# A planned schedule laid out anew: instruction order, PSUM banks and the engines of sixteen operations in a gated linear attention feeding a bilinear FFN

## The chip, the cores and the metric

The kernel runs on one core of one Trainium2 chip. The core has five engines that run side by side, each through its own list of instructions in order: TensorE (PE in the profile, with its weight loads as PEld), VectorE (DVE), ScalarE (ACT), GpSimd (POOL) and SyncE (SP, which here only starts transfers). Transfers are started from the lists of SP, POOL or ACT and carried out by 16 DMA engines. The metric is the device time of one execution in microseconds, and the figure that counts is the median over several runs.

## The reference

Four batches, 8 heads, 768 tokens and 48 channels per head. A recurrent attention with a decay per channel, and then a bilinear feed-forward layer on its output:

```python
for t in range(S):                       # S = 768
    state = alpha[:, :, t, :, None] * state + einsum('bhd,bhe->bhde', k[:, :, t], v[:, :, t])
    y[:, :, t] = einsum('bhd,bhde->bhe', q[:, :, t], state)
x = y.transpose(0, 2, 1, 3).reshape(3072, 384)
out = ((x @ w_a) * (x @ w_b)) @ w_out    # 384 -> 1536 -> 384
```

alpha, q and k lie in float32, and so do the weights; the result is 3072 x 384 in float32.

## The kernel before, in words

**Tiling.** The work is cut into six chunks. Chunk c holds 256 tokens (stripe c // 2 of three) of two batches (u = 0 and 1), so 512 tokens of all heads. A partition holds two neighbouring tokens (r = 0, 1), and the 128 partitions are two halves (g = 0, 1) of 64, over each of which the recurrence is written as a masked product; the state is carried from half to half and from stripe to stripe. So the chunks 2 and 3 need the state left by the chunks 0 and 1, and 4 and 5 that of 2 and 3.

**The stages of one chunk.** Load alpha, k, q and v; take the logarithm of alpha and its running sum on PE; two exponentials of it scale k and q (tile QKp); QKp is turned so that channels lie on partitions (tile kqT); PE forms the scores, the state's update and the output y of the attention; y is brought into the layout of the feed-forward layer (tile xT); PE computes a = x w_a and b = x w_b in twelve pieces of 128 columns each, ACT copies a piece of a out of PSUM, DVE multiplies it with the piece of b that still lies in PSUM (tile prod), and PE multiplies prod by w_out for four blocks m of 128 rows, which are copied out and stored. The chunks 0 and 1 turn QKp on PE and keep y in turned form; chunks 2 to 5 turn both QKp and y by DMA transposes that SP starts.

**What sets the order.** Nothing is planned when the kernel is built. The text `PROGRAM` (line 17 on) lists 837 operations, chunk number first, and the loop at line 921 emits them one after the other. Each engine therefore runs its own operations in the order in which the text names them, and an operation waits for the data it reads and for the buffers it overwrites, however long, with all that follows on the same engine behind it. The last letter of many operations is the engine: V for DVE, S for ACT, P for POOL, Y for SP. A number behind a PE operation is its PSUM bank, of which there are eight; `D`, `SB` and `AQ` take that bank and the next one.

The operations that the text below speaks of, with the function that emits them:

- `ld X u E` (load, line 400): load alpha (a), k, q or v of half-chunk u (`*` both; `0a` and `0b` heads 0 to 3 and 4 to 7 of u = 0). `W` and `Wo` (383, 387): load columns of w_a and w_b, rows of w_out, always from POOL.
- `ln` (408, ACT) logarithm; `l2` (414, POOL or DVE) and `lx` (422, DVE) sum the two tokens of a partition; `H`, `L`, `R` (461, 470, 484) split that sum into parts that PE adds exactly; `B`, `A2`, `AQ` (449, 501, 491) the running sums on PE; `Bs` (456, DVE) that of the even tokens.
- `E` (520, ACT) the exponentials, `i` for k and `b` for q; `ra` (506, ACT) 1/alpha; `lv` (513) the level product, k by alpha or q by 1/alpha, for the even tokens; `mk`, `mq` (535, DVE) the scaled k and q.
- `C`, `Ce` (579, 587) turn QKp on PE and copy it out; `T` (595, SP) the same by DMA; `v` (603) copies a v into the padded tile vx, which only chunks 0 and 1 use.
- `dk`, `de` (558, 567) the decay at the ends of the halves; `K`, `KA` (621, 629) the state's update on PE; `k` (642, DVE) the new state.
- `D` (659) scores; `M` (669, DVE) masks them out of PSUM; `Mc` (673, ACT) copies them unmasked and `Mm` (677, DVE) then masks them in place.
- `SB`, `SA`, `Y` (719, 735) the parts of the attention's output on PE; `X` (748) copies it out of PSUM, and `XT` (762, SP) turns it by DMA for chunks 2 to 5.
- `a f u`, `b f u` (774) one piece of the first layer, `as` (780, ACT) the copy of a, `pr` (786, DVE) the product; the copies of a go round three buffers, so that one waits for the product of the third before it.
- `o m half`, `oc` (794, 805) the second layer; `ot`, `otc` (819, 823) copy it out; `st`, `stc` (832, 835) store it.
- `cu`, `cu2`, `cm`, `ci`, `cz`, `cs`, `c1`, `c2`, `c3` (325 to 376): constants and zeros, nearly all on POOL.

Of the kernel before, what the change touches and what calls it, by code (L numbers as in the profile page):

```python
# [33 lines left out]
1: A2 1 6; ln 0; E 1 b; E 1 i
0: K 1 1 4
1: ld k 1 P
0: Wo 0 6; a 3 1 2; b 5 0 7; k 1 1 V
2: ld a * P
1: l2 0 P
0: cs 1 0 P; Wo 6 12; a 5 1 4; as 5 1; b 5 1 5; pr 5 0; pr 5 1  # L40
1: ra 0; H 0 S; ra 1; L 0 V
0: a 11 * 6; b 3 1 1; as 3 1; pr 3 1; as 11 *; a 4 1 4; as 4 1; a 6 * 0; as 6 *
1: A2 0 2; dk * 3
0: b 11 * 0; pr 11 *; b 6 * 7; pr 6 *; b 4 1 5; pr 4 1
1: lv 0 q P; ld v 1 P
2: ld q * P
1: E 0 i; E 0 b; mq 0 V; lv 0 k V; v 0 V; de *; mk 0 V
0: a 2 1 3; a 10 * 4; as 10 *; b 1 1 7; a 1 1 5; b 7 * 2; b 10 * 1; pr 10 *; a 7 * 6
# [84 lines left out]
2: Mm 0 0 V
1: pr 9 1
2: Y 0; X 0 V; XT 0
3: E 1 b; E 0 b
1: o 0 1 -; ot 0 S; st 2 Y; st 0 Y; a 1 1 0; as 1 1; b 4 1 5; pr 4 1; b 1 1 4; a 8 1 6; as 8 1
0: st 1 Y
3: dr
1: pr 1 1; a 10 1 0; as 10 1; b 8 1 5; b 10 1 2; pr 8 1; pr 10 1; o 3 0 6; o 3 1 -  # L140
3: ld k * P; mq 0 V
4: lx V; ra 0
3: E 0 i; lv 1 k P; lv 0 k P; mk 0 V; T 0
2: b 4 * 0; a 4 * 3; a 10 * 7; b 10 * 4; a 5 * 2; as 10 *; pr 10 *
4: R 0
2: a 2 * 7; as 4 *; pr 4 *; b 5 * 4; a 7 * 1; as 5 *; pr 5 *; b 2 * 3; as 2 *; b 7 * 7; as 7 *; pr 7 *
# [65 lines left out]
4: D 1 0 0; Mc 1 0; Mm 1 0 V; SA 0; Y 0; X 0 S
2: st 2 Y; st 1 Y
4: XT 0
3: o 2 0 7; b 7 * 1
4: Y 1; SA 1
5: AQ 3; E 0 b; E 1 b
3: pr 7 *; o 1 0 2
4: X 1 V; XT 1
3: o 1 1 -; o 2 1 -; o 0 0 0; o 0 1 -  # L220
5: E 0 i; ld q * P; ra 0; E 1 i; mk 1 V; lv 0 q P
3: ot 2 V; st 2 Y
4: a 7 * 4; a 0 * 5; as 0 *; b 0 * 6; b 1 * 7
3: ot 0 S
5: mk 0 V; mq 0 V
3: ot 1 V
5: lv 1 q V; mq 1 V
4: pr 0 *; a 1 * 5; as 1 *; pr 1 *; a 6 * 1; a 2 * 2; as 6 *; as 7 *; as 2 *; b 2 * 6; b 10 * 3; b 6 * 4; b 7 * 0; pr 6 *; pr 7 *; a 10 * 1; as 10 *; pr 10 *
# [17 lines left out]
4: o 3 0 1; o 0 0 7; o 1 0 0; o 0 1 -
5: X 1 S; XT 1
3: st 3 Y
4: o 2 0 2; o 2 1 -; o 3 1 -; o 1 1 -; ot 1 V; st 1 Y; ot 0 S
5: a 3 * 3  # L250
4: ot 3 V
5: b 3 * 7
4: st 3 Y; st 0 Y
5: as 3 *; pr 3 *; a 6 * 5; a 0 * 3; as 0 *; a 1 * 4; as 1 *; b 0 * 1; b 1 * 3; pr 1 *; a 11 * 4; pr 0 *; as 6 *; as 11 *
4: ot 2 S; st 2 Y
5: b 6 * 6; pr 6 *; b 11 * 7; pr 11 *; b 7 * 3; a 8 * 0; a 7 * 5; as 8 *; b 8 * 7; pr 8 *; as 7 *; pr 7 *; b 4 * 2; a 5 * 4; a 4 * 1; a 2 * 7; as 2 *; as 4 *
5: pr 4 *; b 2 * 3; pr 2 *; a 9 * 6; b 5 * 7; as 5 *; a 10 * 1; as 9 *; as 10 *; b 10 * 2; pr 5 *; o 0 0 0; b 9 * 6; pr 10 *; o 3 0 3; pr 9 *; o 0 1 -; ot 0 V
# [699 lines left out]
```

## Time and profile before

| | us |
|---|---|
| median of three runs | 197.73 (197.39 to 216.9) |
| the profiled execution | 196.07 |
| its span, first to last instruction | 194.3 |
| PE busy | 182.1 |
| DVE busy | 135.0 |
| ACT busy | 103.9 |
| POOL busy | 57.0 |

One execution was profiled. Its span is 1.77 us shorter than its own device time, and that device time is 1.66 us below the median. In the rows of the profile a line number such as L778 is the line of the kernel, `out<-in` are tiles, `xN` counts instructions; in the lists in order of time the first number is the start in microseconds after the start of the span and the second the length. A bracket behind a row names the idle time of the engine just before it and what ended it. In the view of the waits, the columns are: in total, how often, the longest.

### The profile page before, as it was taken

The numbers are of one execution on the slowest core, as the hardware profiler recorded it, in microseconds if no ns is written. First come the engines' busy times: TensorE is split into PE (matmuls) and PEld (weight loads), VectorE is DVE, ScalarE is ACT, GpSimd is POOL, SyncE is SP. The second block draws the span as 40 slices with busy tenths as digits, with TensorE's granted clock in tenths as the row PEclk, the third lists the DMA queues.
The fourth block names the chain that finished last, engine by engine and source line by source line (L and its number), as shares of the span: only waits on it lengthen the run. The fifth ranks groups of instructions, "written<-read, shape, count | busy, mean of one in ns | idle before, by whom it ended". The sixth has DMA issues, their size and how long they took to land.

```text
span 194.3 us, 5854 instructions
## 1 busy us (share of the span) xinstructions
PE 182.1 (94%) x2498; PEld 111.3 (57%) x2498; DVE 135.0 (69%) x227; ACT 103.9 (53%) x192; POOL 57.0 (29%) x75
## 2 busy tenths in 40 slices
PE   1798898999989999989999999999999999999993
PEld 1577675666667876634556644555544666544463
DVE  4578845999899898767888289885947770343521
ACT  4558676587736769533445645766154733152510
POOL 7997966830750042600331900000300000000000
PEclk9999999999999999999999999999999999999999
DMA  5999999999899975799987599932797005121004
GB/s 139 241 255 206 244 237 261 256 224 269 204 229 214 179 200 134 76 296 196 201 206 182 117 191 216 126 108 55 85 230 140 3 3 120 43 83 40 0 2 162
DMA packets 57882, 30.96 MB, mean 159 GB/s; under 512 B 47824, under 2 KB 54880, under 8 KB 57856
## 3 DMA queue, kind: packets, MB, share of 16 engines
q0 software_dynamic: 19680, 18.09, 48.5%
q1 hardware_dynamic: 38032, 12.41, 30.6%
q8 instruction: 19, 0.31, 0.7%
q10 hardware_dynamic: 144, 0.10, 0.2%
q14 instruction: 7, 0.06, 0.1%
HBM read 25.98 MB, written 4.74 MB: 158 GB/s over the span
## 4 chain that ended last, share of the span: by engine, by line
PE 77%; DMA 8%; POOL 8%; issue 3%; DVE 2%; ACT 1%; POOLq 0%; DVEq 0%; ACTq 0%
PE psum L778 43%; PE psum L800 22%; DMA wa_t<-in_moe_w_a_dram 5%; DMA xT<-ys 3%; PE psum L666 3%; PE psum L716 2%; POOL a_t L405 2%; PE psum L695 1%; PE psum L619 1%; PE psum L690 1%; PE psum L811 1%; PE psum L499 1%; PE psum L585 1%; POOL wa_t L385 1%; POOL wb_t L385 1%
## 5 line engine op out<-in xcount | busy, mean ns | idle before, releaser
L778 PE MATMUL psum<-xT,wb_t 128*128 128x512 bf16 (+1 forms) x270 | 56.7, 337 | 2.2 <-DMA xT<-ys 1.0
L778 PE MATMUL psum<-xT,wa_t 128*128 128x512 bf16 (+1 forms) x270 | 55.8, 337 | 0.0
L800 PE MATMUL psum<-wo_t,prod 128*128 128x384 bf16 x276 | 48.7, 326 | 0.0
L778 PEld LDWEIGHTS <-wb_t 128*128 128x128 bf16 x270 | 25.5, 98 | 22.6 <-issue 1.7
L778 PEld LDWEIGHTS <-wa_t 128*128 128x128 bf16 x270 | 25.8, 98 | 19.7
L800 PEld LDWEIGHTS <-prod 128*128 128x128 bf16 x276 | 26.1, 98 | 17.6 <-issue 0.6
L518 POOL TENSOR_TENSOR q_t<-q_t,ra 128x384 f32<-128x384 f32 x7 | 7.8, 1117 | 69.0 <-ACT ra L511 51.8
L675 ACT ACTIVATE m<-psum 128x1024 bf16<-128x1024 f32 x16 | 16.0, 1022 | 4.8 <-PE psum L666 4.7
L817 DVE COPY ot<-psum 128x384 f32<-128x384 f32 (+1 forms) x9 | 4.7, 530 | 16.1 <-PE psum L800 15.6
L815 ACT ACTIVATE ot<-psum 128x384 f32<-128x384 f32 (+1 forms) x16 | 7.7, 479 | 14.6 <-PE psum L800 12.0
L544 DVE TENSOR_TENSOR QKp<-k_t,invb 128x768 bf16<-128x768 f32 x10 | 10.0, 997 | 1.7 <-ACT invb L533 1.7
L679 DVE TENSOR_TENSOR m<-m,mask 128x1024 bf16<-128x1024 bf16 x16 | 10.9, 684 | 0.2
L671 DVE TENSOR_TENSOR m<-psum,mask 128x1024 bf16<-128x1024 f32 x8 | 9.7, 1218 | 1.7 <-PE psum L666 1.2
L412 ACT ACTIVATE la<-a_t 128x1536 f32<-128x1536 f32 (+2 forms) x9 | 9.5, 1054 | 2.0 <-DMA a_t<-in_alpha_dram 2.0
L544 DVE TENSOR_TENSOR QKp<-q_t,beta 128x768 bf16<-128x768 f32 x10 | 9.5, 949 | 0.0
L666 PE MATMUL psum<-kqT 64*64 64x128 bf16 x384 | 8.8, 219 | 0.2 <-ACT bl L570 0.2
L454 PE MATMUL psum<-la,ut 128*128 128x192 f32 x16 | 4.7, 446 | 4.2 <-ACT la L412 4.1
L405 POOL DMA_DIRECT2D v_t<-in_v_dram x8 | 8.5, 1065 | 0.3 <-issue 0.2
L405 POOL DMA_DIRECT2D a_t<-in_alpha_dram x7 | 7.4, 1063 | 3.0 <-DMA wa_t<-in_moe_w_a_dram 1.8
L518 POOL TENSOR_TENSOR k_t<-k_t,a_t 128x384 f32<-128x384 f32 x6 | 6.3, 1057 | 6.1 <-DMA k_t<-in_k_dram 6.1
L666 PEld LDWEIGHTS <-kqT 64*64 64x64 bf16 x384 | 6.5, 107 | 2.2 <-issue 2.1
L405 POOL DMA_DIRECT2D k_t<-in_k_dram x7 | 7.4, 1062 | 0.0
(269 smaller groups left out, 274.2 us busy)
## 6 DMA issues: line engine op xcount, KB each, us to landing
out_dram<-ot SPq DMA_DIRECT2D x23, 192.0 KB, 4.1
a_t<-in_alpha_dram POOLq DMA_DIRECT2D x4, 768.0 KB, 12.5
k_t<-in_k_dram POOLq DMA_DIRECT2D x4, 768.0 KB, 7.6
q_t<-in_q_dram POOLq DMA_DIRECT2D x3, 768.0 KB, 8.8
v_t<-in_v_dram POOLq DMA_DIRECT2D x4, 384.0 KB, 6.8
a_t<-in_alpha_dram POOLq DMA_DIRECT2D x3, 384.0 KB, 6.2
k_t<-in_k_dram POOLq DMA_DIRECT2D x3, 384.0 KB, 12.9
q_t<-in_q_dram POOLq DMA_DIRECT2D x3, 384.0 KB, 13.3
```

The lines of the kernel that those rows point to most:

```text
L405: eng.dma_start(out=t[:, us, hs].rearrange("p b h r d -> p (b h) (r d)"), in_=src[ch.b0 + us.start:ch.b0 + us.stop, hs, ch.s * 2 * C:(ch.s ...
L412: nc.scalar.activation(out=ch.la[:, us, hs].rearrange("p b h r d -> p (b h r d)"), in_=ch.a[:, us, hs].rearrange("p b h r d -> p (b h r d) ...
L454: nc.tensor.matmul(p[:, 1], lhsT=ut, rhs=ch.la[:, u, hs, r, :], start=(r == 0), stop=(r == 1))
L518: eng.tensor_mul(x, x, by)
L544: eng.tensor_mul(QKp[ch.c % 2][:, u, j, :, hs, :D], src[:, u, hs].rearrange("p h r d -> p r h d"), f)
L666: nc.tensor.matmul(s2[g * HC:(g + 1) * HC, r, p, rk, :], lhsT=ch.kqT[u][rs, 1, rk, 2 * h + p, g * HC:(g + 1) * HC], rhs=queriesT(ch, u, 2 ...
L671: nc.vector.tensor_mul(m.rearrange("p r a k s -> p (r a) (k s)"), ch.s2[u, h].rearrange("p r a k s -> p (r a) (k s)"), maskn(4))
L675: nc.scalar.activation(out=m.rearrange("p r a k s -> p (r a) (k s)"), in_=ch.s2[u, h].rearrange("p r a k s -> p (r a) (k s)"), func=AF.Copy)
L679: eng.tensor_mul(x, x, maskn(4))
L778: nc.tensor.matmul(p, lhsT=(wa_t, wb_t)[w][:, kk, f * 128:(f + 1) * 128], rhs=ch.xT[:, us.start // 2:us.stop // 2, kk].rearrange("p u g s ...
L800: nc.tensor.matmul(op, lhsT=ch.prod[:, f, at:at + C], rhs=wo_t[:, f, :], start=(f == 0), stop=(f == NFF - 1))
L815: nc.scalar.activation(out=o_, in_=i_, func=AF.Copy)
```

## The change

The functions stay as they are; only `PROGRAM` is another text. It holds the same 837 operations but for the engine or queue of sixteen, and nearly every row of it is in another order and names other banks.

The engines and queues that change (chunk number first):

```
copies:         0: Ce 1 1  V -> S     0: ot 1  V -> S     1: v 0  V -> S     1: v 1  V -> S
                4: X 1     V -> S     4: ot 3  V -> S     5: X 1  S -> V     5: ot 3 S -> V     5: otc 1 1  V -> S
level products: 1: lv 0 q  P -> V     2: lv 0 k  V -> P   3: lv 0 k  P -> V   3: lv 0 q  V -> P   5: lv 0 q  P -> V
loads:          3: ld q *  P -> Y     5: ld q *  P -> Y
```

The order, cut to the places that the prediction uses. The start, with the loads of chunk 0 (half a of the heads first for alpha; k of half b last) and the constants on POOL (the masks, the zeros of the states and the identity moved against the loads):

```diff
-0: c1a; cz 0 q V; cz 0 b P; cu; cu2 P; cs 1 m P; ld a 0b Y; ln 0b; B 0b 6; c1; cz 1 q V; cz 0 v V; Bs 0b; ld a 0a Y; ln 0a; B 0a 2; Bs 0a; fill 5 3; ld k 0b Y
-0: ld q 0b Y; E 0b i; E 0b b; mk 0b V; mq 0b V; cus; E 0a i; E 0a b; ld k 0a Y; mk 0a V; ld q 0a Y; mq 0a V; cm 1; ld v 0 P; v 0 S; ld a 1 P; cm 0; ld v 1 P
-0: ld k 1 P; cs 0 m P; ci; C 0 1 7; Ce 0 1 V; c3 V; C 0 0 0; Ce 0 0 V; fill 1 5; dk 0 5; de 0; K 0 0 7; k 0 0 V; D 0 1 5; M 0 1; D 0 0 0; SB 0 2; ln 1; B 1a 4
...
-0: W a 0 256; X 0 S; C 1 0 7; de 1; Ce 1 0 S
...
+0: c1a; ld a 0a Y; cu; cz 0 v V; cm 0; cz 0 b P; cs 0 0 P; cs 1 0 P; ln 0a; cu2 P; B 0a 6; cz 0 q V; c1; Bs 0a; ld v 0 P; ld a 0b Y; ln 0b; B 0b 4; Bs 0b
+0: fill 5 7; c2 P; ld a 1 P; E 0a i; ld q 0b Y; ld k 0a Y; mk 0a V; E 0b b; E 0a b; mq 0b V; cus; ld q 0a Y; mq 0a V; E 0b i; ld k 0b Y; ld q 1 P; ld k 1 P
+0: ci; mk 0b V; C 0 1 2; Ce 0 1 V; C 0 0 1; Ce 0 0 V; dk 0 7; fill 1 2; v 0 S; de 0; K 0 0 0; k 0 0 V; W b 0 256; ld v 1 P; cz 1 b P; cm 1; D 0 1 5; M 0 1
+0: D 0 0 1; cs 0 m P; SB 0 6; ln 1; B 1a 4; Bs 1a; B 1b 0; Mc 0 0; Mm 0 0 V; Bs 1b; E 1a b; E 1a i; mk 1a V; K 0 1 4; E 1b i; E 1b b; Y 0; SA 0; X 0 S; dk 1 3
+0: de 1; mk 1b V; mq 1a V; C 1 0 1; Ce 1 0 S; mq 1b V; v 1 V; C 1 1 0; Ce 1 1 S; k 0 1 V; K 1 0 7; k 1 0 V; W a 0 256; a 1 0 6; a 0 0 4; b 0 0 3; as 0 0
```

The weights, the second sum over pairs (`1: l2 0`), and the loads around it on POOL. In each text these rows are spread over some twenty; here are POOL's own operations in order, from the first load of weights on:

```
before  0:W a 0 256; 1:ld a 1; 0:W a 256 768; 0:W b 0 256; 0:cz 1 b; 0:W b 256 768; 0:c2; 1:ld a 0; 0:W a 768 1536; 0:W b 768 1536; 1:ld q 0; 1:l2 1; 1:ld v 0; 1:ld k 0; 1:ld q 1; 1:ld k 1; 0:Wo 0 6; 2:ld a *; 1:l2 0; 0:cs 1 0; 0:Wo 6 12; 1:lv 0 q; 1:ld v 1; 2:ld q *; 1:lv 1 q; 1:lv 1 k; 2:ld k *; 3:ld a *
after   0:W b 0 256; 0:ld v 1; 0:cz 1 b; 0:cm 1; 0:cs 0 m; 0:W a 0 256; 1:ld a 1; 0:W a 256 768; 1:ld a 0; 0:W b 256 768; 1:ld k 0; 0:W a 768 1536; 0:W b 768 1536; 1:l2 1; 1:ld q 0; 1:l2 0; 1:ld v 0; 1:ld k 1; 1:ld q 1; 0:cs 1 m; 0:Wo 0 6; 2:ld a *; 0:Wo 6 12; 1:ld v 1; 2:ld k *; 1:lv 1 k; 1:lv 1 q; 2:ld q *; 2:ld v *; 3:ld a *
```

PE's own operations between the last piece of a chunk's attention and the first piece of its first layer:

```
chunk 2  before  2:Y 0; 1:o 0 1; 1:a 1 1; 1:b 4 1; 1:b 1 1; 1:a 8 1; 1:a 10 1; 1:b 8 1; 1:b 10 1; 1:o 3 0; 1:o 3 1; 2:b 4 *
         after   2:Y 0; 1:a 1 1; 1:o 0 1; 1:b 4 1; 1:b 1 1; 1:a 8 1; 1:b 8 1; 1:a 10 1; 1:b 10 1; 1:o 3 0; 1:o 3 1; 2:b 10 *
chunk 3  before  3:Y 1; 2:o 3 0; 2:o 2 0; 2:o 1 0; 2:o 2 1; 2:o 3 1; 2:o 1 1; 3:b 0 *
         after   3:SA 1; 2:o 2 0; 2:o 2 1; 2:o 3 0; 4:AQ; 2:o 3 1; 2:o 1 0; 3:a 0 *
chunk 4  before  4:SA 1; 5:AQ; 3:o 1 0; 3:o 1 1; 3:o 2 1; 3:o 0 0; 3:o 0 1; 4:a 7 *
         after   4:Y 1; 3:o 1 0; 3:o 2 1; 3:o 1 1; 3:o 0 0; 3:o 0 1; 4:b 7 *
```

The end of the program, where the two halves of the last block (`oc 1 0`, `oc 1 1`) and the blocks 2 and 3 change places:

```diff
-5: o 2 0 7; o 3 1 -; ot 3 S; st 3 Y; st 0 Y; o 2 1 -; oc 1 1 0 1; ot 2 V; st 2 Y; oc 1 1 1 -; otc 1 1 V; stc 1 1 S; oc 1 0 0 0; oc 1 0 1 -; otc 1 0 S; stc 1 0 Y
+5: oc 1 0 1 -; o 3 1 -; ot 3 V; st 3 Y; o 2 0 4; otc 1 0 S; stc 1 0 Y; st 0 Y; o 2 1 -; ot 2 V; oc 1 1 0 0; oc 1 1 1 -; otc 1 1 S; stc 1 1 S; st 2 Y
```

More of the change, by code (lines that the diff above doesn't have):

```diff
@@ L34 @@
[L34 to L37, printed above, removed]
-2: ld a * P
[L39 to L48, printed above, removed]
@@ new lines @@
+1: ld a 0 P
+0: W b 256 768
+1: ld k 0 P
+0: W a 768 1536; pr 0 0; D 1 1 0; M 1 1; SB 1 1; W b 768 1536; D 1 0 3; Mc 1 0; b 1 0 5; a 3 0 6; a 4 0 7; pr 1 0; Mm 1 0 V; a 5 0 4
+1: ln 0; l2 1 P
+0: as 3 0
+1: H 1 S; L 1 V
+0: SA 1; Y 1; a 2 0 0
+1: ld q 0 P; l2 0 P; ld v 0 P
+0: b 2 0 6; b 3 0 3; pr 3 0; X 1 S; a 5 1 2
+1: A2 1 1
+0: b 5 0 5; as 2 0
+1: H 0 S
+0: as 4 0; as 5 0
+1: L 0 V
+0: pr 2 0; pr 5 0
+1: ld k 1 P; ld q 1 P
+0: cs 1 m P; Wo 0 6
+2: ld a * P
+0: b 3 1 3; a 3 1 7; as 3 1; b 4 0 6; pr 4 0; K 1 1 5
@@ new lines @@
+0: a 1 1 3; as 1 1; Wo 6 12
+1: ld v 1 P
+2: ld k * P
+1: lv 1 k P; lv 1 q P; mq 1 V; mk 1 V
+2: ld q * P; ld v * P
+3: ld a * P
+0: b 1 1 0; pr 1 1; as 0 1; a 8 * 4; as 8 *; pr 8 *; a 9 * 6; b 9 * 1; b 0 1 2; pr 0 1
+1: C 1 0 0
+0: as 9 *; pr 9 *
+1: D 0 1 3; Mc 0 1
+2: ln *
+1: SB 0 4; D 0 0 6; M 0 0
+0: o 3 0 2
+1: C 1 1 3; Ce 1 1 S
+0: o 0 0 6
+1: SA 0; Mm 0 1 V; Y 0; X 0 S; Ce 1 0 V; D 1 1 0
+0: o 3 1 -; ot 3 S
+1: a 2 0 5
+0: o 0 1 -
+1: Mc 1 1; v 1 S; a 11 0 2; as 11 0; b 11 0 7
+2: lx V; R 0; R 1; AQ 3
@@ L133 @@
[L133 to L146, printed above, removed]
@@ new lines @@
+0: st 3 Y; st 0 Y; st 1 Y
+2: Y 1; X 1 S; XT 1
+1: b 9 1 5; o 0 0 6
+3: AQ 3; E 0 i
+1: ot 2 S
+3: E 0 b
+2: SA 0; Y 0; X 0 V; XT 0
+1: pr 9 1; a 1 1 0; as 1 1
+3: E 1 b
+1: o 0 1 -; b 4 1 7; pr 4 1; ot 0 S; b 1 1 2; pr 1 1; a 8 1 5; b 8 1 1; as 8 1; a 10 1 7; b 10 1 0
+3: ld k * P; lv 1 k P; lv 0 k V
+1: o 3 0 2; pr 8 1; as 10 1; pr 10 1
+3: mq 0 V; dr; E 1 i
+4: ln *; ra 0
+1: o 3 1 -; ot 3 S; st 3 Y
+2: b 10 * 3; a 10 * 5; a 1 * 7; a 2 * 2; as 10 *; as 2 *
+3: mk 0 V; mk 1 V; T 0
+2: pr 10 *
@@ L211 @@
-3: pr 10 *
[L212 to L228, printed above, removed]
@@ L246 @@
[L246 to L257, printed above, removed]
@@ new lines @@
+2: st 3 Y; st 1 Y; st 2 Y; st 0 Y
+4: Mc 1 1
+3: b 3 * 7; pr 3 *; b 10 * 2
+4: SB 1 5; SA 0; D 1 0 0; Mc 1 0; Mm 1 0 V; Y 0; X 0 S; XT 0
+3: o 2 0 7; b 7 * 1
+5: AQ 3
+4: SA 1; Mm 1 1 V; Y 1; X 1 S
+3: pr 10 *
+4: XT 1
+3: o 1 0 2
+5: E 1 b; E 0 i; E 1 i; E 0 b; dr
+3: pr 7 *
+5: mk 0 V; lv 1 q V
+3: o 2 1 -; o 1 1 -; ot 1 V; ot 2 V
+5: ld v * P; lv 1 k P
+3: o 0 0 3; o 0 1 -; ot 0 S
+5: lv 0 q V; mq 0 V; T 0
+4: b 7 * 4; b 2 * 0; b 10 * 3; a 2 * 7; a 0 * 2; as 2 *
+5: mq 1 V; mk 1 V
+4: pr 2 *
```

293 lines of the change are left out of this document (135 added, 158 removed).

## The prediction, as it was made before the result

> **What bounds the kernel now.** I read the page first (which engine is full), then the waits of PE alone, then the busy time by stage, and last the lists in order of time around each wait of PE.
>
> ```profile
> span 194.3 us, 5854 instructions
> PE 182.1 (94%) x2498; PEld 111.3 (57%) x2498; DVE 135.0 (69%) x227; ACT 103.9 (53%) x192; POOL 57.0 (29%) x75
> ...
> PE psum L454 <- ACT la L412: 4.1, 1, 4.1
> PE psum L585 <- POOL ident masks.py:199: 1.2, 1, 1.2
> PE psum L778 <- DMA xT<-ys: 1.0, 1, 1.0
> PE psum L504 <- ACT as__632 L784: 0.8, 1, 0.8
> PE psum L778 <- DVE prod L792: 0.6, 1, 0.6
> PE psum L778 <- DVE Sm L651: 0.5, 1, 0.5
> PE psum L619 <- ACT prod L533: 0.5, 1, 0.5
> PE psum L585 <- DVE QKp L544: 0.2, 1, 0.2
> PE psum L666 <- ACT bl L570: 0.2, 1, 0.2
> ...
> 31.00:55.95 24.95, 24.34 (x374) 16.29 (x371) 22.45 (x37) 16.09 (x31) 12.89 (x12) 1.00 1.20 235
> ```
>
> PE is the bound. It is idle for 194.3 - 182.1 = 12.2 us, and the nine rows of its waits hold 9.1 of these. The first two (5.3 us) are the lead-in, before chunk 0 has anything to turn. What remains, 1.0 + 0.8 + 0.6 + 0.5 + 0.5 + 0.2 + 0.2 = 3.8 us, is all that another order can win behind the lead-in, because PE's matmuls are the same in both texts: 1.9% of the median. From 31 to 55.95 DVE is almost as full as PE (22.45 of 24.95 us), so there it is the next bound. A measurement of this kernel can tell about 2% from no change.
>
> **The change part by part.** I summed PE's work in front of each place in the two texts; the places where a chunk passes from attention to first layer lie at the same amount of work. So I ask only which waits go and which come.
>
> *The lead-in.*
>
> ```profile
> 7.55 0.87 ACT L533 ACTIVATE prod<-psum 128x384 f32<-128x384 f32 x2 [0.40 <-DVE psum L459]
> 7.15 0.37 DVE L459 TENSOR_TENSOR psum<-psum,la 128x192 f32<-128x192 f32 x1 [0.91 <-ACT prod L533]
> 9.01 0.59 POOL masks.py:199 TENSOR_SCALAR_AFFINE_SELECT ident<-ident 128x128 bf16<-128x128 bf16 x1
> 9.66 1.05 PE L585 MATMUL psum<-ident,QKp 128*128 128x128 bf16 x16 [1.24 <-POOL ident masks.py:199]
> ```
>
> Before, the first turn waited for the identity (9.01 + 0.59). After, POOL makes it about 0.5 us sooner, but ACT's four exponentials no longer come in pairs: `E 0a b` stands behind `E 0b b`, which needs the second `Bs` (to 7.52). They end near 8.9 instead of 8.4, and the last product, `mk 0b`, near 9.65: the first turn starts at 9.7, as before. `cs 0 m` moves on POOL behind `cm 1` and ends near 12.3, so `SB 0` starts some 0.3 us later; the waits for bl (0.2; the bank of `dk` is another) and for QKp (0.2; `mk 1b` goes ahead) fall away. Taken: +0.1. Bounds: -0.4 (both waits go, nothing comes) to +0.8 (that and another half microsecond on `SB 0`).
>
> *Chunk 0: weights, and copies on ACT.*
>
> ```profile
> 12.10 0.77 POOL L385 DMA_DIRECT2D wa_t<-in_moe_w_a_dram  x1
> ...
> 13.64 0.76 POOL L385 DMA_DIRECT2D wb_t<-in_moe_w_b_dram  x1
> 14.38 0.52 POOL L348 CAST utr<-ut 128x128 fp32r<-128x128 f32 x1
> L376 POOL MEMSET S<- 128x480 f32 x2 | 1.1, 551 | 0.0
> ...
> wa_t<-in_moe_w_a_dram POOLq DMA_DIRECT2D x1, 384.0 KB, 6.9
> wb_t<-in_moe_w_b_dram POOLq DMA_DIRECT2D x1, 384.0 KB, 8.4
> ...
> L591 ACT ACTIVATE kqT<-psum 128x1024 bf16<-128x1024 bf16 x4 | 4.0, 1022 | 0.3 <-PE psum L585 0.2
> L608 ACT ACTIVATE vx<-v_t 128x768 bf16<-128x768 bf16 x1 | 0.8, 843 | 0.4 <-DMA v_t<-in_v_dram 0.4
> ```
>
> On POOL the middle columns of w_a now stand behind two zeroings of the state (0.55 each), `c2` (0.52) and a load of weights (0.76) that came later before; less one small zeroing that goes, that is some 2.3 us, and 2.4 us for those of w_b. They would land near 14.4 + 6.9 = 21.3 and 16.1 + 8.4 = 24.5, where PE wants them at about 21.1 and 24.0: 0.2 and 0.5 us of waiting if the time to landing holds, less if it was mostly queueing. `Ce 1 1`, now on ACT (1.02 us), stands behind `Ce 1 0`, so `D 1 1` waits some 0.4 us, and `Mc 1 0`, behind both and `ln 1`, holds bank 4 for `a 5 0` by another 0.4. These waits do not add up (PE late for one is in time for the next), and the old 0.5 for Sm goes. Taken: +0.3. Bounds: -0.5 (the old wait goes alone) to +1.5 (all come, one after the other).
>
> *The second sum of chunk 1.*
>
> ```profile
> 26.59 1.17 POOL L405 DMA_DIRECT2D a_t<-in_alpha_dram  x1 [1.84 <-DMA wa_t<-in_moe_w_a_dram]
> 28.82 0.52 ACT L466 ACTIVATE lh<-l 128x384 fp32r<-128x384 f32 x1 [0.92 <-POOL l L420]
> 30.08 0.62 PE psum L504 x2
> ```
>
> `1: l2 0` stood on POOL behind the load of chunk 2's alpha, which waited 1.84 us for an older transfer. ACT waited 0.92 for it with `H 0`, and `as 3 1`, queued behind, freed the bank of `A2 0` late: the 0.8 of the list of waits. After, `l2 0` stands ahead of that load and of four more. Gain: -0.8, bounds -0.8 and 0 (if `ln 0`, now early on ACT, comes as late as the pair sum did).
>
> *Chunk 1: the relief of DVE.* DVE loses `Ce 1 1`, two copies of v, one `ot` and `2: lv 0 k`, and gains one level product, `1: lv 0 q`, earlier.
>
> ```profile
> 52.19 1.35 DVE L518 TENSOR_TENSOR q_t<-q_t,ra 128x384 f32<-128x384 f32 x1
> ...
> 53.93 1.35 DVE L518 TENSOR_TENSOR k_t<-k_t,a_t 128x384 f32<-128x384 f32 x1
> 53.84 1.01 POOL L518 TENSOR_TENSOR k_t<-k_t,a_t 128x384 f32<-128x384 f32 x1
> ...
> L518 DVE TENSOR_TENSOR k_t<-k_t,a_t x4: 548/550/1348, 34.8 to 112.8; 128x384 f32<-128x384 f32 x4
> ```
>
> Three of the five stood between 50 and 56 us in the run of DVE that ended in PE's wait of 0.6 for prod: a copy of v, the copy of an output and the level product of k (1.35 alone). Without them that wait goes: -0.6. But PE is then a microsecond ahead, and DVE is nearly full: `pr 7` behind `mq 0`, `M 0 0` ahead of `o 0 0` and `R 1` ahead of `AQ` come out 0.1 to 0.5 us late. I give +0.5 back. Net -0.1; bounds -0.6 and +0.8.
>
> *From attention to the first layer, chunks 2 to 4.*
>
> ```profile
> 78.05 5.30 DMA xT<-ys
> 107.27 5.99 PE psum L800 x36
> 133.49 0.52 PE psum L499 x12
> ...
> 107.31 0.96 DVE L758 CAST ys<-psum 128x768 bf16<-128x768 f32 x1 [0.86 <-PE psum L716]
> 108.30 1.67 SPq L763 DMA_TRANSPOSE xT<-ys  x1
> ...
> L763 SPq DMA_TRANSPOSE xT<-ys x8: 1213/1255/1924, 75.2 to 162.2; - x8
> DMA to landing us min/median/max: 2.7/2.8/2.8
> L756 ACT ACTIVATE ys<-psum 128x768 bf16<-128x768 f32 x5 | 3.9, 808 | 3.0 <-PE psum L716 1.6 <-PE psum L695 1.3
> ```
>
> In chunk 2 the same ten operations cover the same chain: its wait of 1.0 stays. In chunk 3, copy, transpose and landing took 0.96 + 1.67 + 2.8, with the dispatch 5.5 us, under six half outputs (5.99). Now five of them and `AQ` cover it: 5.0 + 0.52 = 5.5, no slack. In chunk 4 the copy moves to ACT: 0.81 + 1.26 + 2.8 + 0.1 = 5.0 under five half outputs, 5.0: no slack, where `AQ` gave 0.5. Taken +0.2 for both; bounds 0, and +2.4 if both transposes take the 5.30 us of chunk 2 instead of 4.1.
>
> *The rest.* The two loads of q leave POOL for SP. POOL is idle then, so nothing is won; on SP they stand ahead of `dl` and `T`, each one more issue, and the scores that need these lie several microseconds of PE's work later. The other moved copies (chunks 4 and 5) have 7.8 us of outputs over them: 0. At the end, the store of block 2 starts a microsecond later than before but ahead of the last half block, whose path (a copy on ACT, then an issue) is the same: 0, at most +0.5.
>
> **The sum.** +0.1 + 0.3 - 0.8 - 0.1 + 0.2 + 0 = -0.3 us. The profiled execution's 196.07 becomes 195.8. Its runs' median stands 1.66 us higher, at 197.73; so I predict a median of 197.4.
>
> **The rivals.**
>
> 1. *The copy of v on ACT waits for its load* (slower). `1: v 0` now stands on ACT ahead of `ra 1`, `as 11` and both `Ce` of chunk 1, and its load has moved on POOL behind `l2 0`, to about 24.5 us (`ln 0` ends near 23 by my sum of ACT's work, `l2 0` takes about 1).
>
> ```profile
> v_t<-in_v_dram POOLq DMA_DIRECT2D x1, 192.0 KB, 12.3
> ```
>
> By that time to landing v comes at 36.8 us, the copy ends at 37.7, and PE, which by the sum of its work wants it at 35.7 for `KA 0`, waits 2.0 us: 199.4. Against it: those 12.3 us were mostly a queue of older transfers, whose sum in front of v is about the same now, so that it would come near 34.3, 0.5 us in time. It decides from a landing at 34.8 on.
>
> 2. *The transposes of chunks 3 and 4 are slow* (slower): +2.2 over my term, 199.6. For it: chunk 2's took 5.30. Against it: that one ran among two large loads, and chunk 3's took 1.67 + 2.8.
>
> 3. *VectorE and GpSimd block each other.* The level product took 1.35 us on DVE beside one on POOL, and 0.55 (the median) alone. In chunk 3 POOL's `lv 1 k` now falls near DVE's `R 0`, `R 1` and the maskings that lead to chunk 2's transpose, where PE waits already. One such meeting costs 0.8: 198.2. Against it: it needs k to land inside three microseconds. The Trainium skill, "SBUF — State Buffer", section "Who interferes with whom", states that a VectorE instruction with two SBUF inputs contends with a GpSimd instruction that reads SBUF, and that the later one blocks; the 1.35 beside 0.55 agrees with that.
>
> 4. *The waits go and none comes back*: 3.8 us less the 1.0 of chunk 2, 194.9. Against it: DVE's 22.45 of 24.95 us.
>
> **How the numbers follow.** My forecast (195.8 to 198.4) 0.53, rival 1 0.17, rival 2 0.10, rival 3 0.08, rival 4 0.12. Faster by over 2%, under 193.8, needs more than all waits behind the lead-in: 0.05. Slower by over 2%, above 201.7, needs rivals 1 and 2 together or weights and v 4 us late, since the upper bounds add up to 0.8 + 1.5 + 0.8 + 2.4 + 0.5: 0.15. Within: 0.80. The range that leaves out 2 in 10 reaches from rival 4 to a little above rivals 1 and 2: 194.6 to 201.3.
>
> **What would show it.** Right: PE's wait at the second `A2` (L504) and the one for prod near 56 gone, PE 0.5 to 1.5 us ahead at the scores of chunk 2, short waits for xT in chunks 3 and 4, no wait for v on ACT. Wrong: `vx` on ACT (L608) idle before it for a transfer, PE waiting for wa_t or wb_t for a microsecond, a gap over 1 us for xT after 100, or PE idle behind DVE in chunks 2 to 5, where I expect none.

## The result, and the profile after

| | us |
|---|---|
| changed kernel, median of four runs | 207.58 (205.55 to 208.6) |
| kernel before beside it, median of four runs | 198.32 (197.39 to 216.9) |
| ratio after / before | 1.047, 95% interval 1.036 to 1.058 |
| profiled execution of the changed kernel, its span | 207.89, 206.0 |

The change makes the kernel about 9 us slower, outside the range of the forecast. Some executions of several kernels, among them seven of the ten of run 7 below and the profiled one of run 5, came 2 to 10% late for a reason that no trace here shows; the ratios leave these out, the medians don't, so from here on the ratio is the figure to trust.

The page of the changed kernel: span, busy times, and PE's busy row and granted clock in 40 slices of 5.15 us.

```profile
span 206.0 us, 5837 instructions
...
PE 186.4 (90%) x2498; PEld 113.7 (55%) x2498; DVE 134.1 (65%) x223; ACT 107.1 (52%) x197; POOL 52.5 (25%) x72
...
PE   2889999999999589999909989999999999999993
...
PEclk9999999999999969999995999999999999999999
```

The span grew by 11.7 us. PE has the same 2498 matmuls, yet 186.4 - 182.1 = 4.3 us more of busy time; the other 7.4 us are idle. So there are two things to find: a wait, and matmuls that run longer. The clock row has the second: two dips, each just behind a hole in PE's row. The waits of PE have the first:

```profile
PE psum L662 <- DMA kqT<-QKp: 8.4, 3, 4.8
PE psum L450 <- ACT la L408: 4.1, 1, 4.1
PE psum L774 <- DMA xT<-ys: 1.0, 1, 1.0
...
```

The scores (L662) wait 8.4 us for kqT, the tile that SP's DMA transposes `T` write; before, there was no such row. In order of time on PE:

```profile
65.86 0.64 PE L662 MATMUL psum<-kqT 64*64 64x128 bf16 x32 [0.25 <-DMA kqT<-QKp]
...
73.02 0.93 PE L662 MATMUL psum<-kqT 64*64 64x128 bf16 x32 [3.34 <-DMA kqT<-QKp]
73.88 2.10 PE L796 MATMUL psum<-wo_t,prod 128*128 128x384 bf16 x6
...
108.56 0.64 PE L662 MATMUL psum<-kqT 64*64 64x128 bf16 x16 [4.85 <-DMA kqT<-QKp]
```

The kernel before reached its first scores of chunk 2 later:

```profile
68.13 0.64 PE L666 MATMUL psum<-kqT 64*64 64x128 bf16 x32
...
71.45 0.62 PE L666 MATMUL psum<-kqT 64*64 64x128 bf16 x32
```

So at 66 us the changed kernel is 2.3 us ahead. It loses 3.3 us at the scores of u = 0 in chunk 2, and 4.85 us at those of u = 1 in chunk 3. Six half-block matmuls behind the first wait take 2.10 us. Six of the same shape take 1.14 in an undisturbed row of the kernel before:

```profile
97.35 1.14 PE L800 MATMUL psum<-wo_t,prod 128*128 128x384 bf16 x6
```

The busy times by stage (last three columns: granted clock, DMA share, GB/s) show the clock at half behind each wait:

```profile
73.00:76.00 3.00, 2.98 (x46) 1.50 (x50) 1.38 (x2) 1.94 (x2) 0.99 (x1) 0.54 0.07 26
...
103.60:108.50 4.90, 0.11 (x14) 0.01 (x2) 1.48 (x2) 0.00 (x0) 1.20 (x1) 0.88 1.03 255
108.50:111.00 2.50, 2.44 (x21) 1.14 (x22) 0.30 (x1) 1.02 (x1) 0.00 (x0) 0.50 0.22 54
```

While PE waits from 103.6 to 108.5 the DMA engines move 255 GB/s. What they move is on SP's list (two transposes, then the stores, and for chunk 3 one transpose that is issued late) and on POOL's:

```profile
60.76 5.20 SPq L592 DMA_TRANSPOSE kqT<-QKp  x2
66.02 2.15 SPq L829 DMA_DIRECT2D out_dram<-ot  x3
...
91.95 0.46 SPq L401 DMA_DIRECT2D q_t<-in_q_dram  x1
92.47 3.15 SPq L829 DMA_DIRECT2D out_dram<-ot  x2
...
98.07 3.82 SPq L592 DMA_TRANSPOSE kqT<-QKp  x1
```

```profile
62.98 1.96 POOL L514 TENSOR_TENSOR q_t<-q_t,ra 128x384 f32<-128x384 f32 x2 [9.70 <-DMA q_t<-in_q_dram]
64.88 1.19 POOL L401 DMA_DIRECT2D k_t<-in_k_dram  x1
...
98.62 1.00 POOL L514 TENSOR_TENSOR q_t<-q_t,ra 128x384 f32<-128x384 f32 x1 [12.87 <-DMA q_t<-in_q_dram]
99.57 2.36 POOL L401 DMA_DIRECT2D k_t<-in_k_dram  x2
```

On POOL in the kernel before, the k load of chunk 3 stood behind a product that waited for ACT's `ra`:

```profile
68.47 0.99 POOL L518 TENSOR_TENSOR q_t<-q_t,ra 128x384 f32<-128x384 f32 x1 [11.26 <-ACT ra L511]
69.41 1.20 POOL L405 DMA_DIRECT2D k_t<-in_k_dram  x1
...
96.60 2.34 POOL L405 DMA_DIRECT2D k_t<-in_k_dram  x2
```

The time from issue to landing of the transposes `T`, first of the kernel before, then of the changed one. The traces give the landing of only some of the eight in each kernel (two in the changed one, those that PE waited for):

```profile
DMA to landing us min/median/max: 4.3/4.4/5.0
```

```profile
DMA to landing us min/median/max: 9.3/9.9/10.4
```

Chunk 2's second transpose is issued at about 63.7 us and lands at 73.0; the 768 KB of k that POOL issues at 64.9 run beside it. Chunk 3's second is issued at 98.07 and lands at 108.5; 1.5 MB of k are issued from 99.57 on, 1.5 us behind it. Before, the same transpose left SP at 93.45, the k loads followed 3.2 us behind it (96.60), and it landed in 5.0 us:

```profile
93.45 2.71 SPq L596 DMA_TRANSPOSE kqT<-QKp  x1
```

So the first collision is a k load that moved ahead, and the second a transpose that fell back, with three stores now ahead of it on SP.

### The profile page after: what moved, and what is told of

Read it like the earlier page. It is cut to its first block, busy times and chain, and to the rows that moved or that the text cites. A ratio compares the mean times of both kernels' runs of the same rounds, so it can differ in the third digit from the quotient of the medians.

```text
span 206.0 us, 5837 instructions
## 1 busy us (share of the span) xinstructions
PE 186.4 (90%) x2498; PEld 113.7 (55%) x2498; DVE 134.1 (65%) x223; ACT 107.1 (52%) x197; POOL 52.5 (25%) x72
## 4 chain that ended last, share of the span: by engine, by line
PE 81%; DMA 14%; DVE 1%; ACT 1%; issue 1%; DVEq 0%
PE psum L774 44%; PE psum L796 20%; DMA kqT<-QKp 10%; PE psum L662 3%; DMA xT<-ys 3%; PE psum L686 2%; PE psum L712 2%; PE psum L581 2%; PE psum L450 2%; PE psum L615 2%; PE psum L691 1%; DMA a_t<-in_alpha_dram 1%; PE psum L807 1%; PE psum L495 1%; PE psum L561 1%
## 5 line engine op out<-in xcount | busy, mean ns | idle before, releaser
L774 PE MATMUL psum<-xT,wb_t 128*128 128x512 bf16 (+1 forms) x270 | 57.4, 342 | 0.0
L796 PE MATMUL psum<-wo_t,prod 128*128 128x384 bf16 x276 | 50.1, 332 | 0.0
L662 PE MATMUL psum<-kqT 64*64 64x128 bf16 x384 | 10.1, 232 | 8.8 <-DMA kqT<-QKp 8.4
L811 ACT ACTIVATE ot<-psum 128x384 f32<-128x384 f32 (+1 forms) x18 | 8.4, 472 | 13.3 <-PE psum L807 8.2
L675 DVE TENSOR_TENSOR m<-m,mask 128x1024 bf16<-128x1024 bf16 x16 | 11.9, 762 | 4.4 <-ACT m L671 4.3
L662 PEld LDWEIGHTS <-kqT 64*64 64x64 bf16 x384 | 7.3, 113 | 12.0 <-DMA kqT<-QKp 8.9
L514 POOL TENSOR_TENSOR q_t<-q_t,ra 128x384 f32<-128x384 f32 x6 | 6.3, 1055 | 25.7 <-DMA q_t<-in_q_dram 22.9
L540 DVE TENSOR_TENSOR QKp<-k_t,invb 128x768 bf16<-128x768 f32 x10 | 9.4, 948 | 2.1 <-issue 1.5
L529 ACT ACTIVATE beta<-psum 128x384 f32<-128x384 f32 x10 | 5.1, 505 | 4.6 <-PE psum L495 4.6
```

The costliest lines, as they stand in the source:

```text
L514: eng.tensor_mul(x, x, by)
L540: eng.tensor_mul(QKp[ch.c % 2][:, u, j, :, hs, :D], src[:, u, hs].rearrange("p h r d -> p r h d"), f)
L662: nc.tensor.matmul(s2[g * HC:(g + 1) * HC, r, p, rk, :], lhsT=ch.kqT[u][rs, 1, rk, 2 * h + p, g * HC:(g + 1) * HC], rhs=queriesT(ch, u, 2 ...
L675: eng.tensor_mul(x, x, maskn(4))
L774: nc.tensor.matmul(p, lhsT=(wa_t, wb_t)[w][:, kk, f * 128:(f + 1) * 128], rhs=ch.xT[:, us.start // 2:us.stop // 2, kk].rearrange("p u g s ...
L796: nc.tensor.matmul(op, lhsT=ch.prod[:, f, at:at + C], rhs=wo_t[:, f, :], start=(f == 0), stop=(f == NFF - 1))
```

## The experiments

**Theory A**: the transposes are slow because k loads from POOL now run beside them. **Theory B**: they are slow because of what stands on SP's own queue, the q load moved there above all. **Theory C**: the stores right behind them. `gatet u` is an operation that the program already knew (line 850): POOL copies one element of chunk x's turned tile kqT of group u, so that all behind it on POOL waits for that transpose's landing.

**1. The k loads held back.**

```diff
+2: gatet 0
 3: ld k * P; lv 1 k P; lv 0 k V
...
-4: lv 0 q P; R 1; AQ 5; ld k * P; lv 0 k V
+4: lv 0 q P; R 1; AQ 5
+3: gatet 1
+4: ld k * P; lv 0 k V
```

> The changed kernel, with one element of the last transposed tile copied on POOL ahead of the k load of chunk 3, and again ahead of the two k loads of chunks 4 and 5, so that these loads are issued only when the transpose in flight has landed. Theory A (the transposes of chunk 2, group 0, and chunk 3, group 1, are slow because the k loads from POOL share the DMA engines with them): issue to landing falls from about 10 us to under 6 us for both, the waits of the scores for kqT (3.3 and 4.8 us) and the half clock behind them (about 1.5 and 2.7 us by the windows) go: 207.6 - 12.3 = 195.3, up to 199 if the later k loads cost something in chunk 4. Theory B (the transposes are slow because of what stands on SP's own queue, a q load and stores): both waits stay above 2.5 us and the time stays at 204 to 209.

Measured: 200.38 us, ratio to the kernel before 1.012 (1.003 to 1.022). On POOL, and the landing of the transposes:

```profile
68.58 0.46 POOL L851 CAST go<-kqT 1x1 f32<-1x1 bf16 x1 [3.37 <-DMA kqT<-QKp]
68.98 1.20 POOL L404 DMA_DIRECT2D k_t<-in_k_dram  x1
```

```profile
DMA to landing us min/median/max: 4.3/5.1/5.8
```

Nothing on SP was touched, and the transposes land in 4.3 to 5.8 us; both long waits and both clock dips are gone. For these two waits this is theory A, and not B or C. It gave 7.2 us, less than the 8.6 to 12.3 expected: among others, a wait of 1.4 us for kqT came in chunk 4.

**2. The stores ahead.**

```diff
 3: ld q * Y
+0: st 3 Y; st 0 Y; st 1 Y
...
-0: st 3 Y; st 0 Y; st 1 Y
 2: Y 1; X 1 S; XT 1
```

> The changed kernel, with the three stores of chunk 0 that SP issues right behind the transposes of chunk 2 put ahead, right behind the q load of chunk 3 (SP is idle there, 52.6 to 57 us). Theory A (k load from POOL): the transpose of group 0 still takes 8 us or more, the 3.3 us wait stays, 206 to 209. Theory C (the stores behind the transpose on SP's queue share its bandwidth): the transpose takes about 5 us, the first wait and its half clock go, 207.6 - 4.8 = 202.8. The second wait (chunk 3) stays in both.

Measured: 211.39 us, 1.057 (1.046 to 1.069). With no store behind it, chunk 2's second transpose was issued at 65.61 us and PE's wait for it ended at 74.89, 9.3 us later, so C is out. The stores, waiting for their tiles, held SP for 8.97 us, so that the transposes were issued 2.3 us later; a rise over the changed kernel fits that, but the two intervals overlap.

**3. The q loads back on POOL.**

```diff
-3: ld q * Y
+3: ld q * P
...
-5: ld q * Y
+5: ld q * P
```

> The changed kernel, with the q loads of chunks 3 and 5 back on POOL's queue, at the same place in the program: this part of the change undone alone. Theory A (k loads from POOL collide with the transposes): the k load of chunk 3 still follows the product that waits for q, so it stays between 60 and 69 us and the first wait stays over 2 us; the second wait stays as well: 205 to 209. Theory B (the q load on SP's queue holds the transposes up): the first wait and its half clock go, about 202.8, and the second stays, since the q load of chunk 4 was on SP before too.

Measured: 211.3 us, 1.067 (1.059 to 1.075): undoing this part makes it worse. POOL's product, and the k load behind it, moved ahead to 60.2 and 62.8 us; chunk 2's second transpose, issued at 65.24, still kept PE waiting until 73.52, and the second wait stayed too (4.05 us). B is out for these two: the queue of the q load did not cost the time. Neither theory had 211. What rose is a third wait, of 4.2 us instead of 1.0, for xT in chunk 3: its transpose took 8.8 us to land beside a q load and two v loads that POOL issued from 110.7 us on.

**4. The second transpose of chunk 3 early.**

```diff
-3: mq 1 V
+3: mq 1 V; T 1
...
-3: D 0 1 4; M 0 1; SB 0 6; T 1; D 1 0 0
+3: D 0 1 4; M 0 1; SB 0 6; D 1 0 0
```

> The changed kernel, with the second transpose of chunk 3 issued right behind the first, ahead of the q load of chunk 4, three stores and the decay loads; its input is ready on DVE at 91 us. All theories that put the loss into a late issue or into this collision: issued at about 92 instead of 98 us it lands before 99, ahead of the k loads of chunks 4 and 5; the 4.8 us wait and the 2.7 us of half clock go and the first wait stays: 207.6 - 7.5 = 200.1. If the transposes are slow by themselves (about 10 us whatever stands beside them), it lands at about 102 and the wait goes just so; then its issue to landing stays at 10 us. If the loss is elsewhere, 206 to 209.

Measured: 203.69 us, 1.025 (1.014 to 1.035). The second wait for kqT is gone, but only half of the gain stayed: SP's decay load, now behind that transpose, came late, and PE waited for Sm, the state that needs it, and for xT:

```profile
...
PE psum L662 <- DMA kqT<-QKp: 3.7, 1, 3.7
PE psum L691 <- DVE Sm L651: 2.8, 1, 2.8
PE psum L774 <- DMA xT<-ys: 1.9, 1, 1.9
...
```

The first wait, now of 3.70 us, was followed by no half clock here (1.00 in the second row):

```profile
73.36 0.64 PE L662 MATMUL psum<-kqT 64*64 64x128 bf16 x32 [3.70 <-DMA kqT<-QKp]
```

```profile
73.40:76.80 3.40, 3.40 (x109) 2.43 (x110) 1.92 (x3) 2.74 (x3) 0.99 (x1) 1.00 0.07 24
```

**5. PE kept busy in the two gaps.**

```diff
-2: SB 1 3; D 0 1 1; Mc 0 1; D 0 0 5
+2: SB 1 3; fill 12 1; D 0 1 1; Mc 0 1; D 0 0 5
...
-3: D 0 1 4; M 0 1; SB 0 6; T 1; D 1 0 0
+3: D 0 1 4; M 0 1; SB 0 6; T 1; fill 18 0; D 1 0 0
```

> The changed kernel, with dummy products on PE (128x512 of zeros into the bank that the waiting scores write next) ahead of the two score blocks that wait for kqT: 12 ahead of chunk 2, group 0, and 18 ahead of chunk 3, group 1; at 0.215 us each (12 products of this size took 2.75 us in a row of the trace) 2.6 and 3.9 us, less than the waits of 3.3 and 4.8 us. If the half clock behind the waits comes from PE standing idle: the clock row loses its 6 and its 5, the block behind the second wait takes 1.5 instead of 2.7 us, and the time falls by 1.5 + 2.7 to about 203.4. If the low clock has another cause, or the measured loss lies elsewhere: dips stay, 206 to 209.

Measured: 206.82 us, 1.039 (1.025 to 1.054). The transposes landed as late as before (9.1 to 9.6 us), yet the clock stayed at 1.00 from 104 to 113, and PE was far ahead at the running sum of chunk 4. The rows of this run, and then of the changed kernel:

```profile
104.00:113.00 9.00, 8.49 (x177) 4.71 (x175) 5.05 (x6) 4.12 (x4) 4.17 (x4) 1.00 0.58 119
```

```profile
115.62 0.36 PE L495 MATMUL psum<-l,utb 64*64 64x384 bf16 x4
...
121.36 2.19 PE L774 MATMUL psum<-xT,wa_t 128*128 128x512 bf16 x6 [2.98 <-DMA xT<-ys]
```

```profile
119.68 0.37 PE L495 MATMUL psum<-l,utb 64*64 64x384 bf16 x4
...
123.41 1.46 PE L774 MATMUL psum<-xT,wa_t 128*128 128x512 bf16 x6 [0.97 <-DMA xT<-ys]
```

So idleness is what lets the clock fall to half: 4.1 us ahead at 115.6, as expected. The evidence is from the second gap; the first could have passed without half clock, as in run 4. The expected 203.4 did not come: the gain was given back, 2.0 us of it at a wait for xT, whose transposes ran under the v loads from POOL, and more at the half clock behind that wait (six matmuls in 2.19 us).

**6. Chunk 3's ratio late, as before the change.**

```diff
-3: lv 0 q P; ra 1; lv 1 q P
+3: lv 0 q P
...
 2: D 1 0 4; Mc 1 0; D 1 1 6; M 1 1; KA * 30; k * 0 V
+3: ra 1; lv 1 q P
```

> The changed kernel, with chunk 3's second ratio on ACT and the product on POOL that needs it moved to where the kernel before has them, behind the scores of chunk 2, group 1; the k load of chunk 3 stands behind that product on POOL. No wait is added by hand. If the kernel before was spared because this product held its k load back (to 69.4 us there, 64.9 in the changed one): the load is issued at 68 to 70 us, the transpose lands in under 6 us, the first wait and its half clock go, and the second wait stays: 207.6 - 4.8 = 202.8. If the position of the load on POOL doesn't matter: first wait over 2 us, 206 to 209.

Measured: 204.43 us, 1.027 (1.015 to 1.039). No gate, only an old place for one ACT operation and one product:

```profile
67.86 1.00 POOL L515 TENSOR_TENSOR q_t<-q_t,ra 128x384 f32<-128x384 f32 x1 [3.81 <-ACT ra L508]
68.81 1.19 POOL L402 DMA_DIRECT2D k_t<-in_k_dram  x1
```

The first wait fell from 3.3 to 0.2 us; the second stayed (4.0), and a wait of 2.9 us for xT came in chunk 3, which the expected 202.8 did not have. So what had kept k off the transposes of chunk 2 before was a product that waited for `ra`; the new text lets it go at 63 us.

**7 and 8. Both collisions removed by order, and the gated run with one q load moved.** Run 7 against the changed kernel: the first gate of run 1, and

```diff
-4: R 0; ld q * Y
+4: R 0
...
-1: st 0 Y
...
-1: st 2 Y
-3: dl; k * 0 V; k * 1 V
-0: st 2 Y
+3: dl; k * 0 V; k * 1 V; T 1
+4: ld q * Y
+1: st 0 Y; st 2 Y
+0: st 2 Y
...
-5: ld q * Y
...
 4: SB 0 3; T 1; D 1 1 5
+5: ld q * Y
...
+4: gatet 1
 5: ld v * P; lv 1 k P
```

(the old place of chunk 3's `T 1` goes). Run 8: both gates of run 1 and the move of `5: ld q`.

> The changed kernel with both collisions taken out by order: the k load of chunk 3 gated behind the transposes of chunk 2 as in the gated run; on SP chunk 3's decay load and second transpose ahead of the q load of chunk 4 and of three stores (no second gate); the q load of chunk 5 behind chunk 4's transposes, and the v load of chunk 5 gated behind the last of these. Theory A: no wait for kqT over 0.5 us; against the gated run's 200.4 its waits of 1.7 for kqT, 0.5 for Sm and 0.2 go: about 198, between 196 and 199.5, no slower than the kernel before (198.9). If the transposes' own place on SP costs (a late decay load, as in the run with the second transpose early): a new wait for Sm of 1 to 3 us, 199 to 202.

> The gated run (200.4 us) with one thing more: the q load of chunk 5 behind chunk 4's transposes on SP instead of ahead of them. If a large load ahead of a transpose on SP's own queue holds the transpose up: the wait of 1.4 us for kqT in chunk 4 goes: about 199.0. If only POOL's loads do that (v loads of 768 KB are issued there at 111.7 us): the wait stays at 1 us or more and the time at 200 to 201.

Measured: run 7, median of ten 204.18 us, ratio 1.001 (0.991 to 1.011), the profiled execution 196.52; run 8, 199.05 us, 1.001 (0.995 to 1.007). In both the wait for kqT in chunk 4 is gone (run 8: 0.4 us is left, in chunk 2), so a 768 KB load ahead of a transpose on SP's own queue holds it up as well: part of B, in chunk 4. The wait of 1.4 us is what the traces show of it; the 1.3 us between the medians of runs 1 and 8 agree, but their intervals overlap. In both a wait for xT came in chunk 3, under the k loads of chunks 4 and 5, of 2.6 us in run 8 and of 2.4 us in run 7.

**9. The other loads cleared away.** Against run 7, with two one-element copies like `gatet`, one on xT (`gatex`):

```diff
-5: ld k * P
...
 4: lv 1 q P; mq 1 V; mk 1 V
-5: lv 0 k P
+3: gatex 1
...
-4: SB 0 3; T 1; D 1 1 5
-5: ld q * Y
+4: SB 0 3; T 1; D 1 1 5; gatet 1
+5: ld k * P; lv 0 k P; ld q * Y
...
-4: gatet 1
 5: ld v * P; lv 1 k P
```

> The reordered run with its one remaining wait attacked (2.4 us of PE for xT in chunk 3, whose transposes were issued at 101.9 us under two k loads and a v load from POOL): the v load of chunk 4 is gated on POOL behind the landing of chunk 3's second xT transpose, the k load of chunk 5 with its product behind chunk 4's last kqT transpose; the gate on the v load of chunk 5 is dropped, since it follows them. Theory A (any transpose that runs under POOL's loads is slow, those of xT too): the wait falls below 1 us, and the time by 1.5 to 2.4 us against the reordered run's lowest 196.5, to 194 to 195.5, 1 to 2% below the kernel before. If the later loads of chunks 4 and 5 cost as much: new waits for v, k or their products in chunks 4 and 5, 196 to 200.

Measured: 196.91 us, 0.995 (0.989 to 1.001). The gain is smaller than theory A expected (194 to 195.5), and its price elsewhere is plain: chunk 3's wait is gone, but 1.8 us for xT came in chunk 4, under the v load of chunk 5.

**10. The second sum of chunk 1 late again.** Against run 7:

```diff
-1: ld q 0 P; l2 0 P; ld v 0 P
+1: ld q 0 P; ld v 0 P
...
-1: H 0 S
...
-1: L 0 V
...
 2: ld a * P
+1: l2 0 P; H 0 S; L 0 V
```

> The reordered run with chunk 1's second sum of logs (and the two splits that read it) back behind the loads on POOL, as in the kernel before: undoing the step that was priced at 0.8 us. On POOL it moves from 22.6 us behind six issues of 0.9 to 1.2 us, to about 27.6; the product that needs it stood at 27.4 us, so PE should wait there 1.5 to 3.5 us, and reach the scores of chunk 2 at 67 to 69 us instead of 66.0. If that step is worth nothing in this order (a wait behind it takes its place), the scores of chunk 2 stay at 66 to 66.5.

Measured, one run: 208.7 us. PE waits 2.42 us at the decay product (L562), which stands ahead of `A2`, and reaches the scores of chunk 2 at 71.45 us, 5.6 us later than in run 7 (65.85), more than expected and more than the wait: the clock halves here too (0.50 in the second row), and of the 5.6 us, 2.45 are more busy time of PE. The 208.7 has a second part, a wait of 7.2 us for xT in chunk 3, where the later lists collide anew.

```profile
29.44 0.71 PE L562 MATMUL psum<-og,l 128*48 128x2 f32 x25 [2.42 <-ACT as__591 L781]
```

```profile
31.00:32.00 1.00, 1.00 (x6) 0.70 (x6) 0.40 (x1) 0.70 (x3) 0.88 (x1) 0.50 1.17 240
```

**11. The collision put into the kernel before**: its k load of chunk 3 issued when the input of chunk 2's second transpose is written (`gateq`, a one-element copy of QKp).

```diff
-2: T 0
+2: T 0; gateq 0
+3: ld k * P
...
-3: ld k * P; mq 0 V
+3: mq 0 V
```

> The kernel before, unchanged but for one load: chunk 3's k load on POOL is issued as soon as the input of chunk 2's second transpose is written on DVE (one element of it copied on POOL first), so at about 65 us instead of 69.4, right on top of that transpose. Theory A: the transpose takes 8 us or more, PE waits for kqT at the scores that stand at 71.5 us, by some 1.5 to 3 us (an issue at 64.4 plus 9 to 10 us against 71.5), with up to 1.5 us more at half clock: 199.5 to 202.5 against 198. If the loss needs something else of the new order (SP's queue, the copies' engines): within 0.7 us of the kernel before.

Measured: 201.59 us, 1.021 (1.011 to 1.032). One load 4.6 us earlier, and nothing else of the change, gives the kernel before a like wait and a like slow transpose. They fell on the first transpose of chunk 2, not on the second as expected; no half clock followed:

```profile
71.98 0.64 PE L667 MATMUL psum<-kqT 64*64 64x128 bf16 x32 [2.37 <-DMA kqT<-QKp]
```

```profile
DMA to landing us min/median/max: 4.3/4.5/8.4
```

**12. The last one.** Against run 9:

```diff
-5: ld v * P; lv 1 k P
+5: lv 1 k P
+4: gatex 1
+5: ld v * P
```

> The run before this one with all loads cleared away (196.9 us) and its one wait that is left: PE waits 1.8 us for xT in chunk 4, whose transposes are issued at 130.8 us, with the v load of chunk 5 issued from POOL at 132.2 us on top of them. That v load is gated behind their landing. Theory A: the wait falls below 0.7 us and the time by 1.1 to 1.8 us, to 195.1 to 195.8, some 1.2% below the kernel before. If the wait is set by the transposes' own time (two in a row behind the stores): it stays at 1.5 us or more, 196.5 to 197.5.

Measured: 194.22 us, ratio 0.981 (0.976 to 0.987): faster than both kernels, and than the 195.1 to 195.8 expected. Behind the lead-in no wait of PE for a transfer is left:

```profile
span 191.7 us, 5844 instructions
...
PE 182.1 (95%) x2498; PEld 111.6 (58%) x2498; DVE 133.9 (70%) x223; ACT 107.0 (56%) x197; POOL 54.5 (28%) x76
```

```profile
PE psum L452 <- ACT la L410: 4.2, 1, 4.2
PE psum L617 <- ACT prod L531: 0.8, 1, 0.8
PE psum L583 <- DVE QKp L542: 0.6, 1, 0.6
PE psum L664 <- ACT kqT L589: 0.2, 1, 0.2
...
```

PE's busy time is that of the kernel before again, 182.1 us.

## Why the prediction was wrong

*Lead-in, chunks 0 and 1: the right direction, and too small.* The first turn came at 9.64 us (9.7 predicted, 9.66 before). The waits at the second `A2` and for prod near 56 us went, chunk 1's first copy of v on ACT waited for nothing (rival 1 is out), and weights were no wait. The four terms gave -0.5 us at the scores of chunk 2, with 0.5 to 1.5 us ahead as the sign to look for; it was 2.3. PE's work from the first turn to these scores, before and after:

```profile
9.60:68.12 58.52, 55.59 (x913) 40.26 (x912) 48.81 (x92) 39.41 (x83) 31.40 (x36) 1.00 1.17 231
```

```profile
9.60:65.86 56.26, 54.65 (x913) 40.63 (x913) 46.65 (x89) 42.47 (x87) 31.22 (x39) 1.00 1.19 233
```

PE is idle for 2.9 us before and 1.6 after: the waits that the forecast let go went (0.8 at the second `A2`, 0.6 for prod, 0.5 for Sm and 0.2 for QKp among them), and less came back than the terms set aside for new ones. That is 1.3 us instead of 0.5. The other 0.9 are busy time: the same count of matmuls takes 54.65 instead of 55.59 us. No term had this, and no run here shows why. Run 10 adds that the place of the second sum of chunk 1, priced at 0.8, can be worth 5.6 us where POOL's list is the new one.

*"The rest": the step that failed.* It read: "The two loads of q leave POOL for SP. POOL is idle then, so nothing is won; on SP they stand ahead of `dl` and `T`, each one more issue, and the scores that need these lie several microseconds of PE's work later", and costed this at 0. What was wrong was less the moved q loads, which run 3 put back without a gain, than what the step left out. In chunk 2, a product of q on POOL stood ahead of the k load, and with `ra` of chunk 3 earlier it let the k load go 4.5 us sooner, into the transposes (runs 1, 6, 11). In chunk 3 the k loads went 3.0 us later than before, but the transpose went 4.6 us later, and so they met (runs 1, 4). I took the transposes' landing as fixed, "several microseconds" of cover against the 4.4 that the trace showed. Cover of about 6 us was there; beside the k loads they needed 9.3 and 10.4. The step's 0 was a wait of 3.3 and one of 4.85 us.

*The clock.* No term had it. Of the 11.7 us of span, 4.3 are busy time of the same matmuls, and run 5 shows that filling the gaps keeps the clock up. The Trainium skill, "TensorE: Matmul & The Clock Gate", section "What's actually happening", states that after an idle window of some 3.4 us the clock falls to half, until about as long a busy window has passed. The trace agrees for the waits of 3.3 and 4.85 us, with clocks of 0.54 and 0.50 behind them. Behind the 3.70 us of run 4 no half clock followed.

*Rival 2 had the mechanism on the wrong tile.* It let the xT transposes of chunks 3 and 4 take 5.3 us instead of 4.1, "among two large loads", at a price of 2.2 us. The slow ones were those of kqT in chunks 2 and 3, and 5.5 us slower. In runs 7 to 9, once these were free, it came true for xT too (waits of 1.8 to 2.6 us), and in run 3 already (4.2 us).

*Rival 3* did not show: PE's waits behind DVE after 66 us are 0.5 us and less. *Rival 4* (the waits go and none comes back, 194.9) is what run 12 reaches at 194.2, but only with six loads and a transpose in other places.

## What to carry to other kernels

When an order is changed, list what each engine that starts transfers will issue earlier than before, and lay that list over the transfers that PE waits for: an engine "with time to spare" may have been the gate that kept two transfers apart. Price a short transfer by its landing beside a large one, not by its landing alone. A wait of PE of some 2.4 us or more should be priced with a possible loss to the half clock behind it: here none, or about 1.7 us (3.4 us at half clock), or 2.8 us behind the wait of 4.85 (5.6 us of busy time at half clock).

## What the runs showed of the hardware that was not expected

- A DMA transpose of 128 x 2048 bf16 elements of QKp lands 4.3 to 5.0 us after its issue in the kernel before, 4.3 to 5.8 where the k loads were held back (runs 1 and 8), and 8.4 to 10.4 beside one or two k loads of 768 KB from POOL; putting six loads and a transpose elsewhere is worth 13 us here (207.6 against 194.2). The Trainium skill, "DMA: Bandwidth & Descriptors", section "SWDGE vs HWDGE vs iDMA", states that the queues fed from GpSimd and from SP are served in turn by the same DMA engines; the stretched landing agrees, though no run here shows the turns themselves.
- Behind idle times of PE of as little as 2.42 us (run 10), 2.83 (run 4) and 2.98 (run 5) the clock fell to half, while behind 2.40 (run 7), 2.64 (run 8), 2.71 (run 3), 2.87 (run 6) and even 3.70 (run 4) it did not. So in this case the length of a gap alone does not decide. The Trainium skill, "TensorE: Matmul & The Clock Gate", section "What's actually happening", gives an idle window of some 3.4 us; the three gaps that half clock followed are shorter than that. What the traces' clock records show besides: between the first turn and the end, each stretch of half clock lasts 3.41 or 6.83 us, and within a run these begin a whole number of 3.41 us apart (at 73.22 and 107.36 us in the changed kernel, ten times 3.41; at 30.23 and 118.98 in run 10, 26 times). That would fit a clock that is set anew every 3.41 us by what PE did in the stretch before, so that it counts where in it a gap falls; no run here moved a gap to test this.
